# The opening of an FNet and SwiGLU kernel: a warm-up without ScalarE, a first tile negated by VectorE, roots tile by tile, whole first blocks

## The chip, the cores and the metric

The kernel runs on one core of a Trainium2 chip. TensorE multiplies, VectorE and ScalarE do elementwise work, GpSimd does small steps and issues some transfers, and SyncE (SP) issues the others. The metric is the time on the device in microseconds (us), lower is better. Beside it stands one profiled execution, whose trace gives the start and length of each instruction.

## The reference, cut to what matters

```
xn = layernorm(x)                                   # x: 2048 x 640
a, b = xn @ hid_re.T, xn @ hid_im.T                 # DFT along the hidden dimension, 640
s = seq_re @ a - seq_im @ b                         # DFT along the sequence, 2048 (real part)
g = silu((silu(xn @ w_gate) * (xn @ w_up)) @ w_down)   # 640 -> 1536 -> 640
out = x + s * g
```

All is float32.

## The kernel before

The sequence DFT is done first: the two 2048 x 2048 matrices times the normalised rows, result in p_dram. Then the hidden DFT (y_dram), then the feed-forward part in two halves of the sequence, and the product with y and the sum with x at the end. Each of the large products is one level of Strassen's scheme: seven products p1 to p7 of quarter matrices, plus the products d1 to d3 for the last 128 of the 640 columns.

A float32 product is made of faster ones: each operand is split into a rounded high part (ScalarE copies it to a type called fp32r) and a low part (VectorE subtracts the high part from the original). Each 128x128 by 128x512 product is then three matmuls: high by high, high by low, low by high (`mm3`). Only the first products of the opening take unsplit float32 operands.

All work is collected in a `Plan`: matmul groups are steps at planned times from 0 on, and everything else is given a planned time ahead of, or behind, the step that it serves. `schedule` sorts all this; `place` then gives each buffer an address in one of the arenas hl (split operands), raw (everything else) and raw2, by trying five orders of the buffers and several distances in time, `fit` placing one buffer after another. Instructions are then issued in planned order. Each engine works through its own list in order, so a planned time decides what stands ahead of what on an engine, and an instruction that waits holds up those behind it.

The opening (`opening`, within `seq`) covers the first eight row tiles (kk = 0 to 7, 128 rows each). For each tile kk it has two groups of products: the real block (i = 0) and the imaginary block (i = 1) of the sequence DFT, each with three matmul targets, two of p1 and one of d1. For tile 0 they are unsplit: the right operand is `neg`, the negated first 256 columns of the tile, and the tile's own last 128 columns. From tile 1 on each group is nine matmuls. Which block comes when is written by hand:

- the transfers, all in SP's list: x tile 0, first half of real block 0, x tile 1, first half of imaginary block 0, then the two second halves, x tiles 2 and 3, and so on; a half block is 256 KB, a block 512 KB (two k tiles of 128x512), an x tile 320 KB;
- `OPEN_LN`: planned times for the layer norm of tiles 0, 1, 2 with 3, 4 with 5, 6 with 7: statistics on VectorE, a square root on ScalarE, five small steps on VectorE (a reciprocal, then a Newton step that gives the reciprocal root r, then the shift mr), then the normalisation in place on ScalarE;
- `OPEN_T` and `OPEN_S`: planned times for the splits of the right operands (per tile) and of the left ones (per block).

Before all that, z is cleared, ScalarE applies one square root to an element of z, so that its table is loaded, and sixteen matmuls of z with itself (`busy`) run ahead of the first real one. They keep TensorE at work while the first data come in.

Of the kernel before, what the change touches and what calls it, by code (L numbers as in the profile page):

```python
# [11 lines left out]
AF = mybir.ActivationFunctionType  # L12
ALU = mybir.AluOpType

P = 128
S, D, F = 2048, 640, 1536
TC = 512
# [79 lines left out]
class Plan:  # L97
# [97 lines left out]
    def place(self, limits, last):  # L195


        self.ops.sort(key=lambda o: o[:2])
        life = {}
        for i, (t, _, _, names, end) in enumerate(self.ops):  # L200
            for n in names:
                if n in self.size:
                    v = life.setdefault(n, [t, i, end, i])
                    v[2:] = max(end, v[2]), i
        where = {}
        turn = max(v[3] for n, v in life.items() if self.size[n][0] == "raw2")
        free = max(v[2] for n, v in life.items() if self.size[n][0] == "raw2")
        back = next(i for i, o in enumerate(self.ops) if o[0] >= self.back)
        for arena, limit in limits.items():
            wall = {"hl": [(limit, limit + last[0], turn, free + 1, 1e9), (limit + last[0], limit + sum(last), turn, free + 1, back)],  # L210
                    "raw": [(limit, limit + last[1], back, self.back + 2, 1e9)]}.get(arena, [])
            limit = max([limit, *(w[1] for w in wall)])
            mine = [(n, self.size[n][1], *v) for n, v in life.items() if self.size[n][0] == arena]
            orders = (
                lambda m: (m[2], m[3]),
                lambda m: (m[4] - m[2] < 60, m[2], m[3]),
                lambda m: (m[4] - m[2] < 60, -m[1], m[3]),
                lambda m: (-m[1], m[3]),
                lambda m: (m[2] - m[4], m[3]),
            )  # L220
            pauses = (8, 6, 4, 3, 2, 1, 0, -1, -2, -4, -8)
            tries = ((pauses[a:], o) for a in range(len(pauses)) for o in orders)
            found = [f for f in (self.fit(sorted(mine, key=o), limit, p, wall) for p, o in tries) if f]
            if not found:
                raise ValueError(f"{arena}: no room")
            best = min(found, key=lambda f: f[0])
            order, latest = best[3], best
            for _ in range(24):
                hurt = sorted((n for n in latest[2] if latest[2][n] > 9), key=lambda n: -latest[2][n])
                moved = {n: i for i, n in enumerate(hurt[:6])}  # L230
                order = sorted(order, key=lambda m: moved.get(m[0], 99))
                latest = next((f for f in (self.fit(order, limit, pauses[a:], wall) for a in range(len(pauses))) if f), None)
                if latest is None:
                    break
                best = min(best, latest, key=lambda f: f[0])
            where |= best[1]
        return where, turn + 1, back
# [33 lines left out]
def tile_fnet_swiglu(  # L271
# [278 lines left out]
    def xn_tiles(k, n, a=0, w=D):  # L550
        return space["xn", k // 8].rearrange("p (k d) -> p k d", d=D)[:, k % 8:k % 8 + n, a:a + w]
# [7 lines left out]
    def layer_norm(k0, n, lead, root, stats, small):  # L559

        for k in range(k0, k0 + n):
            for h in range(2):
                pl.prod(stats[k - k0], lambda k=k, h=h: nc.vector.bn_stats(
                    bst[:, k % 2, h], xn_tile(k)[:, h * 320:h * 320 + 320]), [(xn, k)], [("bst", k % 2, h)])
            pl.prod(stats[k - k0], lambda k=k: nc.vector.bn_aggr(
                mv[:, k], bst[:, k % 2].rearrange("p a b -> p (a b)")),
                [("bst", k % 2, 0), ("bst", k % 2, 1)], [("mv", k)])  # L570
        y, t, mr, v, nm = (sm[:, i, k0:k0 + n] for i in range(5))
        mean, var = (mv[:, k0:k0 + n, i] for i in range(2))
        r = rowst[:, 0, NS + k0:NS + k0 + n]
        key = ("sm", k0)
        if small is nc.vector:
            stt = small.scalar_tensor_tensor
            ops = [
                lambda: nc.scalar.activation(t, var, AF.Sqrt, bias=sm[:, 5, :1]),
                lambda: small.reciprocal(y, t),
                lambda: stt(t, var, EPS, y, op0=ALU.add, op1=ALU.mult),  # L580
                lambda: stt(t, t, -0.5, y, op0=ALU.mult, op1=ALU.mult),
                lambda: stt(r, t, 1.5, y, op0=ALU.add, op1=ALU.mult),
                lambda: stt(mr, mean, -1.0, r, op0=ALU.mult, op1=ALU.mult),
            ]
        else:
            ops = [
                lambda: small.tensor_scalar(v, var, EPS, 1.0, op0=ALU.add, op1=ALU.mult),
                lambda: small.tensor_tensor(y, v, sm[:, 5, 8:8 + n], op=ALU.pow),
                lambda: small.tensor_scalar(nm, mean, -1.0, 0.0, op0=ALU.mult, op1=ALU.add),
                lambda: small.tensor_tensor(t, v, y, op=ALU.mult),  # L590
                lambda: small.tensor_tensor(t, t, y, op=ALU.mult),
                lambda: small.tensor_scalar(t, t, -0.5, 1.5, op0=ALU.mult, op1=ALU.add),
                lambda: small.tensor_tensor(r, y, t, op=ALU.mult),
                lambda: small.tensor_tensor(mr, nm, r, op=ALU.mult),
            ]
        for i, fn in enumerate(ops):
            pl.prod(root[i > 0], fn, [("mv", k) for k in range(k0, k0 + n)], [key])
        for k in range(k0, k0 + n):
            pl.prod(lead[k - k0], lambda k=k: nc.scalar.activation(
                xn_tile(k), xn_tile(k), AF.Identity, bias=sm[:, 2, k:k + 1], scale=rowst[:, 0, NS + k:NS + k + 1]),  # L600
                [key, (xn, k)], [(xn, k, c) for c in range(3)])
# [86 lines left out]
    def more():  # L688
# [9 lines left out]


    OPEN_LN = ((0, 1, -4.0, -2.8, -2.6, (-1.4,)), (1, 1, -1.4, 0.0, 0.3, (1.4,)), (2, 2, 2.2, 5.8, 5.9, (7.0, 9.0)),  # L700
               (4, 2, 10.5, 13.0, 13.1, (14.2, 17.0)), (6, 2, 18.5, 21.0, 21.1, (22.5, 25.0)))
    OPEN_T = {1: 2.4, 2: 8.0, 3: 10.1, 4: 15.2, 5: 18.0, 6: 23.5, 7: 26.2}
    OPEN_S = {(0, 1): (0.2, 1.6), (1, 1): (0.8, 3.9), (0, 2): (4.6, 7.2), (1, 2): (8.7, 9.4), (0, 4): (13.5, 14.5),
              (1, 4): (15.8, 16.8), (0, 6): (21.5, 22.5), (1, 6): (24.0, 25.2)}
    ahead = {}

    def seq(k):
# [112 lines left out]
        def opening():  # L820
# [16 lines left out]
                else:  # L837
                    pl.prod(at(t), lambda: nc.sync.dma_start(raw(name, a * TC, TC), src[:, a]), [], [(name, a)])

            t = -8.0  # L840
            for what in ((0,), (0, 0, 0), (1,), (1, 0, 0), (0, 0, 1), (1, 0, 1), (2,), (3,), (0, 1), (1, 1), (4,), (5,), (0, 2), (1, 2),
                         (6,), (7,), (0, 3), (1, 3)):
                if len(what) == 1:
                    load_x(what[0], at(t), nc.sync)
                else:
                    fetch(what[0], what[1], t, *what[2:])
                t += 0.45
            for k0, n, stats, root, rest, apply in OPEN_LN:
                layer_norm(k0, n, [at(x) for x in apply], (at(root), at(rest)), [at(stats + i) for i in range(n)], nc.vector)
            neg = pl.buf(("neg",), "raw", 256)  # L850
            pl.prod(at(-0.5), lambda: nc.scalar.activation(
                raw(neg).unsqueeze(1), xn_tiles(0, 1, 0, 256), AF.Copy, scale=-1.0), [(xn, 0, 0)], [(neg, 0)])
            for kk in range(1, 8):
                for r, late in (("p1", 0), ("d1", 0.4)):
                    LEAD["T" + r, kk] = 0, at(OPEN_T[kk] + late), at(OPEN_T[kk] + late + 0.5)
# [469 lines left out]
    found, turn, back = pl.place({"hl": HL_KB * 256, "raw": RAW_KB * 256 - 8, "raw2": TURN_KB * 512}, (TURN_KB * 256, TURN_KB * 256))  # L1325
    where.update(found)

    nc.gpsimd.memset(sm[:, 5, :8], EPS)
    nc.gpsimd.memset(sm[:, 5, 8:], -0.5)
    nc.gpsimd.memset(z, 0.0)  # L1330
    nc.scalar.activation(z[:, :1], z[:, :1], AF.Sqrt)
    started = False
    first, last = ExitStack(), ExitStack()
    for i, stack in enumerate((first, last)):
# [1 line left out]
    for i, (t, _, fn, names, _) in enumerate(pl.ops):  # L1336
        if i == turn:
            last.close()
            first.close()
            space["hl2"], space["hl3"] = (stack.enter_context(tc.tile_pool(name=name, bufs=1, reuse_waits="tile")).tile(  # L1340
                [P, TURN_KB * 256], F32R, name=name) for stack, name in ((ctx, "hl2"), (last, "hl3")))
        if i == back:
            last.close()
            space["raw3"] = ctx.enter_context(tc.tile_pool(name="raw3", bufs=1, reuse_waits="tile")).tile(
                [P, TURN_KB * 256], F32, name="raw3")
        if t >= 0 and not started:
            started = True
            busy(ps[:, 7], 16)
        fn()


# [38 lines left out]
```

## Time and profile before

| | us |
|---|---|
| median of 3 runs (fastest to slowest) | 971.04 (971.01 to 1213.72) |
| the profiled execution, its own time | 971.28 |
| its span, first to last instruction | 969.5 |
| first warm-up matmul | 2.28 |
| first real matmul | 8.39 |
| first matmul on split operands | 13.14 |

The span is what the trace covers; the profiled execution's own time is 1.8 us longer. All rows are in microseconds from the start of the span, unless a column says ns. PE is TensorE, PEld its weight loads, DVE VectorE, ACT ScalarE, POOL GpSimd, and SPq SyncE's issue of transfers. Nearly every instruction is recorded by a helper, so all have line L82, and the tile names tell them apart: xn is the row tiles, sm and rowst the small per-row numbers of the layer norm, raw the plain buffers, hl the split ones, ps the accumulators, in_cs the sequence DFT matrices.

### The profile page before, as it was taken

To read this page: it belongs to the slowest core of one execution; us is meant where nothing else is said; L and a number is where in the kernel's file an instruction comes from. 1 tells how busy PE (TensorE), PEld (TensorE's weight loads), DVE (VectorE), ACT (ScalarE), POOL (GpSimd) and SP (SyncE) were. 2 spreads that over 40 slices of the span, in tenths; PEclk is the share of its full clock that TensorE was granted. 3 is DMA by queue.
4 is the path that set the end of the run, shared out by engine and by line. 5 is a ranking of instruction groups with operands and counts; after the bars stand their busy time and mean duration, and the time that the engine had idled before them with its cause. 6 is when DMAs were issued, how large, how long until landed. Compare 5 with 4: busy or idle time off the path is not lost.

```text
span 969.5 us, 11543 instructions
## 1 busy us (share of the span) xinstructions
PE 962.3 (99%) x4240; PEld 792.9 (82%) x4240; DVE 733.9 (76%) x927; ACT 489.3 (50%) x676; POOL 119.5 (12%) x179
## 2 busy tenths in 40 slices
PE   9999999999999999999999999999999999999997
PEld 5888888888888888888888888888888888888886
DVE  6899688666874687685987888999977666667774
ACT  5786455454555446544346556563445444444341
POOL 0460220011101110111100211210002100000000
PEclk9999999999999999999999999999999999999999
DMA  9998858395838488678573474438688511105593
GB/s 338 289 228 260 220 178 229 114 255 140 212 126 247 136 218 297 155 202 233 160 220 124 159 267 155 168 135 285 227 276 251 145 55 55 37 18 194 196 363 125
DMA packets 64344, 186.50 MB, mean 192 GB/s; under 512 B 6560, under 2 KB 10400, under 8 KB 64288
## 3 DMA queue, kind: packets, MB, share of 16 engines
q1 hardware_dynamic: 46240, 125.45, 38.3%
q0 software_dynamic: 18048, 60.32, 24.4%
q8 instruction: 33, 0.54, 0.2%
q14 instruction: 23, 0.19, 0.1%
HBM read 151.39 MB, written 34.36 MB: 192 GB/s over the span
## 4 chain that ended last, share of the span: by engine, by line
PE 99%; ACT 0%; DVE 0%; issue 0%
PE ps L82 99%; ACT L82 0%; DVE raw L82 0%; ACT raw L82 0%; ACT z L82 0%
## 5 line engine op out<-in xcount | busy, mean ns | idle before, releaser
L82 PE MATMUL ps<-hl 128*128 128x512 f32 (+1 forms) x3277 | 787.9, 388 | 0.0
L82 PEld LDWEIGHTS ps<-hl 128*128 128x128 f32 x3277 | 613.9, 188 | 127.0 <-issue 0.2
L82 DVE TENSOR_TENSOR hl<-raw,hl 128x1024 fp32r<-128x1024 f32 (+5 forms) x360 | 346.6, 994 | 137.2 <-ACT hl L82 92.9
L82 ACT ACTIVATE hl<-raw 128x1024 fp32r<-128x1024 f32 (+6 forms) x416 | 325.8, 826 | 169.2 <-DVE raw L82 91.7
L82 PE MATMUL ps<-hl,hl 128*128 128x512 f32 (+1 forms) x935 | 257.5, 388 | 0.0
L82 ACT ACTIVATE raw<-ps 128x512 f32<-128x512 f32 (+1 forms) x144 | 97.7, 681 | 235.3 <-PE ps L82 230.6
L82 DVE TENSOR_TENSOR raw<-raw 128x256 f32<-128x256 f32 (+7 forms) x236 | 193.0, 843 | 18.3 <-ACT raw L82 15.2
L82 PEld LDWEIGHTS ps<-hl,hl 128*128 128x128 f32 x935 | 175.3, 188 | 36.1
L82 DVE TENSOR_TENSOR raw<-ps,raw 128x512 f32<-128x512 f32 (+1 forms) x95 | 77.2, 814 | 50.9 <-PE ps L82 50.1
L82 ACT ACTIVATE hl<-xn 128x1024 fp32r<-128x1024 f32 (+3 forms) x61 | 42.4, 723 | 13.0 <-PE ps L82 10.2
L82 POOL DMA_DIRECT2D p_dram<-raw x24 | 16.4, 685 | 248.5 <-DVE raw L82 210.3
L82 ACT ACTIVATE raw<-raw 128x512 f32<-128x512 f32 (+1 forms) x30 | 21.5, 718 | 45.9 <-DVE raw L82 44.6
L82 DVE TENSOR_TENSOR hl<-xn,hl 128x1024 fp32r<-128x1024 f32 (+3 forms) x50 | 40.8, 833 | 3.6 <-PE ps L82 3.5
L82 POOL DMA_DIRECT2D raw<-in_cs x36 | 32.2, 987 | 77.6 <-DMA raw<-in_cs 45.6
L82 DVE SCALAR_TENSOR_TENSOR hl<-raw,hl 128x256 fp32r<-128x256 f32 (+4 forms) x56 | 32.8, 586 | 4.2 <-ACT hl L82 4.2
L82 POOL DMA_DIRECT2D out<-raw x10 | 6.9, 685 | 225.0 <-DVE raw L82 189.4
L82 DVE TENSOR_TENSOR raw<-raw,raw 128x512 f32<-128x512 f32 (+3 forms) x30 | 29.0, 973 | 4.7 <-ACT raw L82 4.1
L82 POOL DMA_DIRECT2D d_p<-hl x28 | 15.2, 543 | 71.3 <-ACT hl L82 60.1
L82 DVE BATCH_NORM_STATS2 bst<-xn 128x6 f32<-128x320 f32 x32 | 13.7, 480 | 5.0 <-DMA xn<-in_x 5.0
L82 POOL DMA_DIRECT2D y_dram<-raw x12 | 8.2, 682 | 64.8 <-DVE raw L82 46.4
L82 POOL DMA_DIRECT2D raw<-in_xt x6 | 6.9, 1210 | 72.1 <-DVE raw L82 72.1
L82 ACT ACTIVATE xn<-xn,sm,rowst 128x640 f32<-128x640 f32 x16 | 14.2, 912 | 3.0 <-DVE sm L82 2.0
(38 smaller groups left out, 86.7 us busy)
## 6 DMA issues: line engine op xcount, KB each, us to landing
raw<-in_cs SPq DMA_DIRECT2D x82, 512.0 KB, 6.0
hl<-d_p SPq DMA_DIRECT2D x56, 384.0 KB, 5.2
raw<-in_cs POOLq DMA_DIRECT2D x36, 512.0 KB, 9.2
raw<-in_wb SPq DMA_DIRECT2D x24, 640.0 KB, 4.2
d_p<-hl POOLq DMA_DIRECT2D x28, 384.0 KB, 3.4
p_dram<-raw POOLq DMA_DIRECT2D x16, 512.0 KB, 3.7
raw<-p_dram SPq DMA_DIRECT2D x8, 768.0 KB, 6.9
xn<-in_x SPq DMA_DIRECT2D x16, 320.0 KB, 8.8
```

The lines of the kernel that those rows point to most:

```text
L82: return real(*args, **kw)
```

## The change

The opening is rewritten in five places.

1. z is cleared first, and ScalarE's first square root reads and writes a small tile instead of z. The dummy matmuls wait for the memset alone, and there are eleven of them.
2. For tile 0, VectorE subtracts the mean and multiplies with the negative reciprocal root, straight from the loaded tile, into `neg`; the last 128 columns get the same with the positive root, in place; ScalarE normalises the first 512 columns later. The separate sign flip on ScalarE is gone.
3. Tiles 0 to 3 get their roots one by one. ScalarE computes t, half the root of var + eps; GpSimd computes (var + eps) / 4; VectorE takes the reciprocal of t, one combined step, and a second reciprocal that gives r. Tiles 4 to 7 keep the old steps in pairs.
4. Blocks 0 are fetched whole, and SP's list is two entries shorter.
5. The planned times of the opening are new, and `place` gets additional orders for the case that none of the old ones finds room.

```diff
             found = [f for f in (self.fit(sorted(mine, key=o), limit, p, wall) for p, o in tries) if f]
+            for w in range(25, 425, 25) if not found else ():
+                order = sorted(mine, key=lambda m: (m[4] - m[2] < 60, m[2] < w, m[2], m[3]))
+                found += [f for f in (self.fit(order, limit, pauses[a:], wall) for a in range(len(pauses))) if f]
...
-        if small is nc.vector:
+        if small is nc.vector and n == 1:
+            sign, half = (-1.0, nm) if k0 == 0 else (1.0, r)
+            ops = [
+                lambda: nc.scalar.activation(t, var, AF.Sqrt, bias=sm[:, 5, 4:5], scale=0.25),
+                lambda: nc.gpsimd.tensor_scalar(v, var, EPS, 0.25 * sign, op0=ALU.add, op1=ALU.mult),
+                lambda: small.reciprocal(y, t),
+                lambda: small.scalar_tensor_tensor(v, v, y, t, op0=ALU.mult, op1=ALU.subtract if k0 == 0 else ALU.add),
+                lambda: small.reciprocal(half, v),
+            ]
+            if k0:
+                ops.append(lambda: small.scalar_tensor_tensor(mr, mean, -1.0, r, op0=ALU.mult, op1=ALU.mult))
+        elif small is nc.vector:
...
+        if k0 == 0:
+            neg = pl.buf(("neg",), "raw", 256)
+            minus = lambda to, a, n, scale: small.tensor_scalar(to, xn_tile(0)[:, a:a + n], mean, scale, op0=ALU.subtract, op1=ALU.mult)
+            for e in range(2):
+                pl.prod(root[2], lambda e=e: minus(raw(neg, e * P, P), e * P, P, nm), [(xn, 0), key], [(neg, 0)])
+            pl.prod(root[2], lambda: small.tensor_scalar(r, nm, -1.0, 0.0, op0=ALU.mult, op1=ALU.add), [key], [key])
+            pl.prod(root[2], lambda: minus(xn_tile(0)[:, TC:], TC, P, r), [(xn, 0), key], [(xn, 0, 2)])
+            pl.prod(root[2], lambda: small.tensor_tensor(mr, mean, nm, op=ALU.mult), [key], [key])
+            pl.prod(lead[0], lambda: nc.scalar.activation(
+                xn_tile(0)[:, :TC], xn_tile(0)[:, :TC], AF.Identity, bias=mr, scale=r), [key, (xn, 0), (neg, 0)], [(xn, 0, 0), (xn, 0, 1)])
+            return neg
...
-    OPEN_LN = ((0, 1, -4.0, -2.8, -2.6, (-1.4,)), (1, 1, -1.4, 0.0, 0.3, (1.4,)), (2, 2, 2.2, 5.8, 5.9, (7.0, 9.0)),
-               (4, 2, 10.5, 13.0, 13.1, (14.2, 17.0)), (6, 2, 18.5, 21.0, 21.1, (22.5, 25.0)))
-    OPEN_T = {1: 2.4, 2: 8.0, 3: 10.1, 4: 15.2, 5: 18.0, 6: 23.5, 7: 26.2}
-    OPEN_S = {(0, 1): (0.2, 1.6), (1, 1): (0.8, 3.9), (0, 2): (4.6, 7.2), (1, 2): (8.7, 9.4), (0, 4): (13.5, 14.5),
+    OPEN_DMA = ((0,), (0, 0), (1,), (1, 0), (2,), (3,), (0, 1), (1, 1), (4,), (5,), (0, 2), (1, 2), (6,), (7,), (0, 3), (1, 3))
+    OPEN_LN = ((0, 1, (-2.5,), (-1.4, -1.0, -0.5), (0.4,)),
+               (1, 1, (0.5,), (1.6, 1.9), (2.8,)),
+               (2, 1, (3.4,), (4.5, 4.9), (5.7,)),
+               (3, 1, (6.6,), (7.65, 9.3), (10.1,)),
+               (4, 2, (10.5, 11.5), (13.0, 13.1), (14.2, 17.0)),
+               (6, 2, (18.5, 19.5), (21.0, 21.1), (22.5, 25.0)))
+    OPEN_T = {1: 3.7, 2: 6.7, 3: 11.0, 4: 15.2, 5: 18.0, 6: 23.5, 7: 26.2}
+    OPEN_S = {(0, 1): (-1.1, 2.8), (1, 1): (1.3, 5.8), (0, 2): (4.7, 7.6), (1, 2): (7.7, 10.2), (0, 4): (13.5, 14.5),
...
-            t = -8.0
-            for what in ((0,), (0, 0, 0), (1,), (1, 0, 0), (0, 0, 1), (1, 0, 1), (2,), (3,), (0, 1), (1, 1), (4,), (5,), (0, 2), (1, 2),
-                         (6,), (7,), (0, 3), (1, 3)):
+            t = -6.0
+            for what in OPEN_DMA:
...
-            neg = pl.buf(("neg",), "raw", 256)
-            pl.prod(at(-0.5), lambda: nc.scalar.activation(
-                raw(neg).unsqueeze(1), xn_tiles(0, 1, 0, 256), AF.Copy, scale=-1.0), [(xn, 0, 0)], [(neg, 0)])
...
-    nc.gpsimd.memset(sm[:, 5, :8], EPS)
+    nc.gpsimd.memset(z, 0.0)
+    nc.gpsimd.memset(sm[:, 5, :4], EPS)
+    nc.gpsimd.memset(sm[:, 5, 4:8], 0.25 * EPS)
     nc.gpsimd.memset(sm[:, 5, 8:], -0.5)
-    nc.gpsimd.memset(z, 0.0)
-    nc.scalar.activation(z[:, :1], z[:, :1], AF.Sqrt)
+    nc.scalar.activation(sm[:, 0, :1], sm[:, 5, :1], AF.Sqrt)
...
-            busy(ps[:, 7], 16)
+            busy(ps[:, 7], 11)
```

## Rows read from the trace of the kernel before

**Rows 1.** The page: busy time, share of the span and instructions of each engine.

```profile
PE 962.3 (99%) x4240; PEld 792.9 (82%) x4240; DVE 733.9 (76%) x927; ACT 489.3 (50%) x676; POOL 119.5 (12%) x179
```

**Rows 2.** Waits of PE: us in total, times, longest us.

```profile
PE ps L82 <- ACT z L82: 2.3, 1, 2.3
```

**Rows 3.** Order of time on PE: start, us, engine, operation, count, idle time before.

```profile
2.28 6.27 PE L82 MATMUL ps<-z 128*128 128x512 bf16 x16 [2.28 <-ACT z L82]
8.39 1.88 PE L82 MATMUL ps<-raw 128*128 128x512 f32 x4
...
13.14 373.46 PE L82 MATMUL ps<-hl 128*128 128x512 f32 x1645
```

**Rows 4.** Order of time, all engines, first 14 us: the clearing and use of z.

```profile
0.80 0.53 POOL L82 MEMSET z<- 128x512 bf16 x1
...
2.02 0.20 ACT L82 ACTIVATE z<-z 128x1 bf16<-128x1 bf16 x1
```

**Rows 5.** Order of time, first 14 us: weight loads of the last warm-up matmuls.

```profile
7.38 0.15 PEld L82 LDWEIGHTS <-z 128*128 128x128 bf16 x1 [0.28 <-issue]
7.74 0.31 PEld L82 LDWEIGHTS <-z 128*128 128x128 bf16 x2 [0.21 <-issue]
```

**Rows 6.** Order of time, first 14 us: tile 0, from its landing to its negated copy.

```profile
3.54 0.89 DVE L82 BATCH_NORM_STATS2 bst<-xn 128x6 f32<-128x320 f32 x2 [3.54 <-DMA xn<-in_x]
...
4.71 0.29 ACT L82 ACTIVATE sm<-mv,sm 128x1 f32<-128x1 f32 x1 [2.48 <-DVE mv L82]
...
5.04 0.16 DVE L82 RECIPROCAL sm<-sm 128x1 f32<-128x1 f32 x1 [0.36 <-ACT sm L82]
...
5.82 0.16 DVE L82 SCALAR_TENSOR_TENSOR sm<-mv,rowst 128x1 f32<-128x1 f32 x1
...
6.96 0.42 ACT L82 ACTIVATE raw<-xn 128x256 f32<-128x256 f32 x1
```

**Rows 7.** Groups by form, first 40 us: count, busy us, mean ns, idle before.

```profile
L82 DVE TENSOR_TENSOR hl<-xn,hl 128x128 fp32r<-128x128 f32 x8 | 2.2, 273 | 0.0
...
L82 DVE TENSOR_TENSOR hl<-raw,hl 128x512 fp32r<-128x512 f32 x2 | 1.4, 688 | 0.3 <-ACT hl L82 0.3
```

**Rows 8.** Order of time on POOL: small layer norm steps of later tiles.

```profile
42.20 0.18 POOL L82 TENSOR_SCALAR sm<-mv 128x2 f32<-128x2 f32 x1 [1.90 <-DVE mv L82]
...
43.99 1.04 POOL L82 TENSOR_SCALAR sm<-sm 128x2 f32<-128x2 f32 x1
```

**Rows 9.** Order of time, first 14 us: what waited for transfers, and tile 1.

```profile
6.37 0.89 DVE L82 BATCH_NORM_STATS2 bst<-xn 128x6 f32<-128x320 f32 x2 [0.40 <-DMA xn<-in_x]
...
8.44 0.63 ACT L82 ACTIVATE hl<-raw 128x512 fp32r<-128x512 f32 x1 [0.61 <-DMA raw<-in_cs]
...
10.04 0.63 ACT L82 ACTIVATE hl<-raw 128x512 fp32r<-128x512 f32 x1 [0.96 <-DMA raw<-in_cs]
...
10.57 0.91 ACT L82 ACTIVATE xn<-xn,sm,rowst 128x640 f32<-128x640 f32 x1
...
10.83 0.89 DVE L82 BATCH_NORM_STATS2 bst<-xn 128x6 f32<-128x320 f32 x2 [1.03 <-DMA xn<-in_x]
...
11.96 0.42 DVE L82 SCALAR_TENSOR_TENSOR hl<-xn,hl 128x256 fp32r<-128x256 f32 x1
```

**Rows 10.** Stretches: us, busy us (instructions) by engine, PE clock, DMA share, GB/s.

```profile
5.00:10.00 5.00, 5.00 (x15) 2.06 (x13) 3.40 (x14) 2.26 (x5) 0.00 (x0) 1.00 0.97 263
10.00:15.00 5.00, 5.00 (x16) 2.72 (x15) 3.94 (x14) 3.30 (x6) 0.00 (x0) 1.00 1.03 418
```

**Rows 11.** Order of time, 14 to 30 us: low parts for tile 2.

```profile
16.59 0.43 DVE L82 SCALAR_TENSOR_TENSOR hl<-xn,hl 128x256 fp32r<-128x256 f32 x1 [0.31 <-ACT hl L82]
...
17.75 1.23 DVE L82 TENSOR_TENSOR hl<-raw,hl 128x1024 fp32r<-128x1024 f32 x1 [0.53 <-ACT hl L82]
```

**Rows 12.** Waits of SP's own queue: us in total, times, longest us.

```profile
SPq L82 <- DVE hl L82: 284.3, 45, 25.8
```

**Rows 13.** The page, DMA issues: count, KB each, us to landing.

```profile
raw<-in_cs SPq DMA_DIRECT2D x82, 512.0 KB, 6.0
```

More of the change, by code (lines that the diff above doesn't have):

```diff
@@ L847, in opening @@
                 t += 0.45
-            for k0, n, stats, root, rest, apply in OPEN_LN:
-                layer_norm(k0, n, [at(x) for x in apply], (at(root), at(rest)), [at(stats + i) for i in range(n)], nc.vector)
-            neg = pl.buf(("neg",), "raw", 256)
-            pl.prod(at(-0.5), lambda: nc.scalar.activation(
-                raw(neg).unsqueeze(1), xn_tiles(0, 1, 0, 256), AF.Copy, scale=-1.0), [(xn, 0, 0)], [(neg, 0)])
+            neg = [layer_norm(k0, n, [at(x) for x in apply], [at(x) for x in root], [at(x) for x in stats], nc.vector)
+                   for k0, n, stats, root, apply in OPEN_LN][0]
             for kk in range(1, 8):
```

## The prediction

> **What bounds the kernel now.** I read three views in this order. First the busy times of the page: TensorE is busy for 962.3 of 969.5 us, and no other engine comes near [rows 1]. A busy matmul row alone doesn't prove a bound, so the second view is what the matmuls waited for: over the whole execution there is one wait, 2.3 us at the start, for ScalarE [rows 2]. Third, the order of time on TensorE: warm-up matmuls from 2.28, the first real ones from 8.39, and from 13.14 products of split operands that follow each other without a gap [rows 3]. So the time is 8.39 us of opening, then some 956 us of unbroken matmuls, then a tail of about 5 us. The change touches the opening. Whatever it brings is at most what lies ahead of 8.39, and it counts in full only if the matmuls behind find their operands that much earlier as well.
>
> What fills the 8.39 us: ScalarE loads its table, and its first activation, in place on z, ends at 2.22; z itself was written by 1.33 [rows 4]. Sixteen warm-up matmuls follow, 0.43 us apart (512 columns in 0.43 us is the 1.2 GHz level); the weight loads close up from 0.43 to under 0.4 us at 7.74, which is where the 2.4 GHz level begins [rows 5]. That is about 5.4 us after the first of them. Meanwhile the first tile's negated copy is ready at 6.96 + 0.42 = 7.38 [rows 6]. So the real matmuls start when the warm-up ends, 1 us after their operands exist.
>
> **The change, part by part.** *Warm-up.* The dummy matmuls need only z. Its memset takes 0.53 us [rows 4] and now goes first in GpSimd's list, so they start at about 1.35, 0.9 us earlier. Eleven at 0.43 us end at 6.05.
>
> *First operand.* It no longer passes through ScalarE's normalisation and sign flip. VectorE subtracts the mean and multiplies by the negative root itself. From the square root's end at 5.00 [rows 6]: reciprocal, one combined step, reciprocal, each 0.16 us as there and 0.2 us from start to start, until 5.6; then two subtractions of 128x128, for which the nearest row is a 128x128 tensor operation of 0.27 us [rows 7]. That makes 6.15, 1.2 us earlier than 7.38. The added GpSimd step (variance plus eps) runs beside the square root. Its nearest rows are 0.18 us and, beside a VectorE operation, 1.04 us [rows 8]. At 4.7 VectorE waits for ScalarE, as it does in the first of those rows, so I take 0.18 and it is hidden; at 1.04 it would end at 5.75 and the operand would come 0.5 us later.
>
> *First left operand.* The first seq-DFT block is now fetched as one 512 KB transfer instead of its first half. Landing times of before, by the engines that waited for them: x tile 0 at 3.54 [rows 6], x tile 1 at 6.37, the second half of block 0 at 8.44, the second half of the imaginary block 0 at 10.04, x tile 2 at 10.83 [rows 9]. In the order of issue these stand after 320, 896, 1408, 1664 and 1984 KB. The whole block 0 now stands at 832 KB: between 3.54 and 6.37 that is 6.06; at the 418 GB/s of the later stretch [rows 10] it is 4.8. Either is ahead of 6.15. So the first real matmul can start at 6.2 against 8.39, 2.2 us earlier.
>
> *Clock.* If the faster level again comes 5.4 us after the first dummy, that is 6.75, and the stretch from 6.2 to 6.75 runs at half pace: it costs 0.3 us. If it came at 7.7 as before, it would cost 0.75; if before 6.2, nothing. I take 0.3. The first three unsplit products are six records of 0.43 us, 2.56 us, so they end at 6.2 + 2.56 + 0.3 = 9.05.
>
> *Second left operand.* The next three products need the imaginary block 0, now whole, at 1664 KB. By the bytes of before it lands at 10.04; at 418 GB/s, 1376 kB after 3.54, at 6.85. The 5 to 10 us stretch moved 263 GB/s [rows 10], which gives 8.8. I take that, as it is the stretch in question. Then TensorE doesn't wait: 9.05 + 2.56 = 11.6 against about 13.5 before, where twelve records from 8.39 end.
>
> *Second tile.* Here I expect most of the gain to be lost. ScalarE works in order, and its new list puts the split of the imaginary block (now 0.63 us, after the landing) ahead of the square root of tile 1; before, that root was ahead of both splits. So: split 8.8 to 9.45, root from 9.45. Then from the root's start to the shift's end took 4.71 to 5.98 for tile 0 [rows 6] with five VectorE steps, now four: 1.1 us, to 10.55. Normalising takes 0.91 [rows 9], to 11.5, and the rounded (high) part of its right operand 0.42, as the flip of the same size did [rows 6]: 11.9. On VectorE the low part of the same operand stands behind the low part of block 0 (0.69 [rows 7], to 11.25) and behind the statistics of tile 2 (10.83 to 11.96 before, 1.15 us to the next operation [rows 9], so to 12.4), and takes 0.42: 12.8. The third matmul of the group needs it, 0.45 us after the first, so the group runs as if started at 12.35. Against 13.5 the gain is 1.15 us. The root's fewer steps are worth 0.2 us per tile, and only for tile 1 do they lie on this path. Tiles 2 and 3, now one by one, add five small steps (1 us) to VectorE, which was busy 3.4 and 3.9 of each 5 us [rows 10].
>
> *Behind that.* The tightest operands of the old opening are the low part of tile 2's right operand, ready at 17.02 for a matmul at 18.05, and the low part of the next imaginary block, ready at 18.98 for 19.85 (start of the second tile's group at 13.5 plus two or three groups of nine matmuls at 0.227 us, 2.04 each, plus one or two matmuls) [rows 3, 11]. They have 1.0 and 0.9 us. A gain of 1.15 us therefore asks little more of them than they had, and both chains begin earlier now, tile 2's without waiting for tile 3. I cost this at nothing; if they didn't move at all, the gain would end at 0.9.
>
> Sum: -1.15 us on the profiled execution of 971.28 us, which lies 0.24 above the median of the runs shown; from that median, 971.04, I get **969.9**.
>
> **Rivals.** *The transfers decide.* The block lands no earlier than 10.04 by bytes and tile 2 not before 10.83. Then the split ends at 10.7, the root's chain at 11.8, the high part at 13.15, the low part at 14.0; the group runs as from 13.6 and nothing is gained: 971.0. For it: the DMA was as busy in 5 to 10 us as later, yet slower [rows 10]. Against it: those were 256 KB pieces; whole blocks ran at 418 GB/s.
>
> *The best case.* The block lands near 7 and the clock rises early. Then TensorE alone decides, 6.2 + 5.12 = 11.3, a gain of 2.2: 968.8. Against it: the statistics of tile 2 ahead of tile 1's low part.
>
> *The clock (slower).* Before, TensorE worked without a break from 2.28 to the rise, and on. Now eleven dummies end at 6.05, perhaps before the rise, and any pause until the operand, or until the second block, interrupts that work. If the 5.4 us then start anew at 6.2, the products up to 11.6 run at half pace and lose 2.7 us: they end at 14.0, 0.5 us later than before, 971.5. It decides as soon as the pause resets the rise. Against it: the pause I compute is 0.15 us. The Trainium skill, "TensorE: Matmul & The Clock Gate", section "What's actually happening", speaks against shortening the warm-up: it says that the monitor runs freely and isn't reset by the kernel's start, so that the rise comes at a varying moment. By that rule the price would differ from run to run between 0 and the 0.75 us above, and the runs before should scatter too; two agree within 0.03 us, so I give it little.
>
> *Placement (slower).* The planner gets additional orders for the case that no old order finds room; if one of them is used, buffers of the whole kernel change place, and some transfer is issued only when its buffer comes free. The SP queue already waited 284.3 us in 45 waits for VectorE to be done with a buffer, 6.3 us each [rows 12], without TensorE noticing. A block needs 6.0 us from issue to landing [rows 13], and 1.2 us for its low part [rows 11]: a buffer that comes free less than about 7 us before its use stops TensorE. A few such cases at 1 to 2 us give 973 or so.
>
> **Numbers.** Forecast (gain 0.5 to 2.2, its own range 968.8 to 970.5, best case within): 0.60. Transfers decide, 970.5 to 971.2: 0.20. Clock, 971.5: 0.06. Placement, 971.2 to 975, seldom far more: 0.12. Still faster: 0.02. The range 968.8 to 971.6 leaves out the last and most of placement. A measurement tells about 2% (19 us) from no change; the opening has only 8.39 us to give, so faster by that much is all but excluded (0.01), slower needs many placement stalls (0.02), within 2% 0.97.
>
> **What would show it.** The first dummy near 1.35, the first unsplit product near 6.2, the first split product between 11.9 and 12.4, no matmul waits behind it. A weight-load pace of 0.85 us among the unsplit products would be the clock; a ScalarE split that waits for its block until 10 the transfers; TensorE gaps behind 60 us placement.

## The result and the profile after

The changed kernel takes 974.17 us (median of 8 runs, 973.58 to 974.73) against 971.02 for the kernel before: ratio 1.0032, 95% interval 1.0021 to 1.0044. It is 3.1 us slower. One of the eight runs of the kernel before took 1213.72 us, which nothing on record explains, and the ratio leaves it out. The prediction had it 1.1 us faster, with 968.8 to 971.6 as its range.

First the order of time on TensorE after, to be read against [rows 3] (start, us, then the instruction):

```profile
1.30 4.68 PE L82 MATMUL ps<-z 128*128 128x512 bf16 x11 [1.30 <-POOL sm L82]
6.48 1.98 PE L82 MATMUL ps<-raw 128*128 128x512 f32 x4 [0.49 <-DVE raw L82]
...
9.25 1.98 PE L82 MATMUL ps<-raw 128*128 128x512 f32 x4
...
12.41 47.82 PE L82 MATMUL ps<-hl 128*128 128x512 f32 x208 [0.32 <-ACT hl L82]
```

The dummies start 1 us earlier, the first real matmul 1.9 us earlier, the split products 0.7 us earlier. So in this pair of executions the opening did what it was meant to do. The waits of TensorE in the whole execution (us in total, times, longest), against the single one of [rows 2]:

```profile
PE ps L82 <- DVE hl L82: 2.5, 1, 2.5
PE ps L82 <- POOL sm L82: 1.3, 1, 1.3
PE ps L82 <- DVE raw L82: 0.5, 1, 0.5
PE ps L82 <- ACT hl L82: 0.3, 1, 0.3
```

Three of the four belong to the opening. The first doesn't. It lies at 743 us, where the second half's gate products begin. Among VectorE's waits stands one that the kernel before doesn't have, for output transfers:

```profile
DVE raw L82 <- DMA out<-raw: 6.8, 2, 5.9
```

The order of time there, all engines:

```profile
728.62 1.24 POOL L82 DMA_DIRECT2D raw<-in_xt  x1 [21.29 <-DVE raw L82]
...
739.46 0.74 POOL L82 DMA_DIRECT2D out<-raw  x1 [9.60 <-DMA raw<-y_dram]
...
743.25 0.61 PE L82 MATMUL ps<-hl,hl 128*128 128x512 f32 x2
744.54 0.83 DVE L82 TENSOR_TENSOR raw<-raw 128x640 f32<-128x640 f32 x1 [5.86 <-DMA out<-raw]
...
745.89 0.42 DVE L82 SCALAR_TENSOR_TENSOR hl<-raw,hl 128x256 fp32r<-128x256 f32 x1
...
746.36 4.38 PE L82 MATMUL ps<-hl,hl 128*128 128x512 f32 x11 [2.50 <-DVE hl L82]
```

VectorE stands idle for 5.86 us, until an output transfer that GpSimd issued at 739.46 has landed. That transfer waits in turn for the one issued at 728.62, which adds x to what stands in the same buffer (an accumulating transfer). The view puts this wait to a load of y; but the output instruction itself waits on the semaphore of the accumulating transfer, which landed at 739.2, 0.3 us earlier, and in the kernel before the two stand 0.3 us apart as well. VectorE's next operation forms the weight sums of the first column block, and behind it in VectorE's order stands the low part that TensorE's third matmul of this stage needs. In the kernel before, the same VectorE operation (there merged with the one after it) doesn't wait, although the output transfer was issued at the same time:

```profile
739.18 1.42 DVE L82 TENSOR_TENSOR raw<-raw 128x640 f32<-128x640 f32 x2
739.58 0.74 POOL L82 DMA_DIRECT2D out<-raw  x1 [9.07 <-DMA raw<-in_xt]
```

The stretches after (us, busy us and instructions of PE, PEld, DVE, ACT, POOL, then PE's granted clock, DMA share, GB/s):

```profile
743.00:746.00 3.00, 0.86 (x4) 0.38 (x2) 1.46 (x3) 0.60 (x2) 0.00 (x0) 1.00 0.98 157
746.00:750.00 4.00, 3.64 (x9) 2.92 (x10) 4.00 (x8) 3.76 (x7) 1.66 (x2) 0.57 0.35 114
750.00:754.00 4.00, 4.00 (x20) 3.21 (x19) 4.00 (x9) 2.51 (x6) 0.28 (x1) 1.00 0.50 109
```

TensorE issues 4 matmuls in the 3 us of the gap and 9 in the next 4 us at a granted clock of 0.57. The kernel before has 15 and 19 there.

To see what is left of the opening just before this, take one VectorE operation, the same in both kernels, first of before, then of after:

```profile
724.25 1.22 DVE L82 TENSOR_TENSOR hl<-raw,hl 128x1024 fp32r<-128x1024 f32 x1
```

```profile
723.61 1.22 DVE L82 TENSOR_TENSOR hl<-raw,hl 128x1024 fp32r<-128x1024 f32 x1
```

The changed kernel is 0.64 us ahead at 724 us. Matmul by matmul (both traces have all 4212 products on split operands) it then loses 2.66 us in the gap and 1.72 us behind it, so the last matmul comes 3.74 us later; the tail behind the last matmul is 0.75 us shorter in this execution, and the span is 3.0 us longer (972.5 against 969.5).

Why the two kernels differ at 743 us, with no code changed there: the new planned times of the opening change how long its buffers live, and `place` then finds another arrangement. For the hl arena none of the five old orders finds room any more, and one of the additional orders is used. For the raw arena the arrangement that the kernel before had no longer fits, and the next best is taken. In it the result buffers of three quarters of the first half's down product (12, 22 and 21) are reused 2.0 to 3.4 us of planned time after their planned end; in the kernel before nothing follows any of them within 8.8 us. These buffers wait for an accumulating transfer on GpSimd's queue and then for the output transfer, and both land later than the planner assumes: it counts 4.4 and 3.4 us from issue to landing, and for quarter 12 they took 10.6 and 5.0.

### The profile page after: what moved, and what is told of

Read it like the earlier page. It is cut to its first block, busy times and chain, and to the rows that moved or that the text cites. A ratio compares the mean times of both kernels' runs of the same rounds, so it can differ in the third digit from the quotient of the medians.

```text
span 972.5 us, 11526 instructions
## 1 busy us (share of the span) xinstructions
PE 963.7 (99%) x4235; PEld 792.6 (81%) x4235; DVE 734.0 (75%) x932; ACT 488.7 (50%) x676; POOL 120.2 (12%) x184
## 4 chain that ended last, share of the span: by engine, by line
PE 93%; issue 4%; DMA 1%; POOL 0%; DVE 0%; ACT 0%; SPq 0%; POOLq 0%; DVEq 0%
PE ps L82 93%; DMA raw<-in_cs 1%; DMA out<-raw 1%; POOL raw L82 0%; DVE raw L82 0%; SPq L82 0%; ACT xn L82 0%; POOL out L82 0%; DVE sm L82 0%; ACT hl L82 0%; DVE hl L82 0%; ACT raw L82 0%; ACT sm L82 0%; DVE rowst L82 0%; POOLq L82 0%
## 5 line engine op out<-in xcount | busy, mean ns | idle before, releaser
L82 DVE TENSOR_TENSOR raw<-raw 128x1024 f32<-128x1024 f32 (+6 forms) x233 | 193.9, 856 | 28.0 <-ACT raw L82 13.5
L82 PEld LDWEIGHTS ps<-hl,hl 128*128 128x128 f32 x945 | 178.3, 189 | 39.9 <-DVE hl L82 2.9
L82 DVE TENSOR_TENSOR raw<-raw,raw 128x256 f32<-128x256 f32 (+3 forms) x33 | 28.4, 866 | 5.5 <-ACT raw L82 5.1
L82 ACT ACTIVATE xn<-xn,sm,rowst 128x640 f32<-128x640 f32 (+1 forms) x16 | 14.2, 908 | 5.0 <-DVE sm L82 3.4
```

Of the source, the lines that this page charges most:

```text
L82: return real(*args, **kw)
```

## The experiments

Each comparison is with runs of the kernel before taken beside it on the same chip, so the time of that kernel is given with it.

**One buffer moved in the changed kernel.**

```diff
     where.update(found)
+    where["fin", 0, 12, 0, 0] = 14336
```

> The changed kernel with one address changed: the result buffer of quarter 12 of the first half's down product is put at word 14336 of the raw arena, which is free for its whole life, instead of at word 6528, where the weight sums of the second half's first column block are written next. Theory (the address costs the time): VectorE no longer waits 5.86 us for the output transfer, TensorE's gap of 2.66 us at 743 us and the slow matmuls behind it (1.7 us) go, nothing else changes: 974.2 - 4.4 = 969.8 us, and the opening's gain of 0.64 us over the kernel before is left, plus what its tail differs. Rival (the earlier opening makes TensorE run ahead of its transfers, whatever the addresses): the wait turns up at another buffer at about the same place, and the time stays at 973 to 974.5.

Measured: 973.71 us against 971.25, ratio 1.0026 (1.0015 to 1.0037). The 5.86 us wait at 744 is gone, yet most of the loss stayed, as the rival had it. In the profiled execution three gaps, of 0.7 to 0.8 us lost at each, took its place: one at 731, for a load of the down product's d3 operand, and two at 750 and 770. One row of its order of time shows where the last comes from:

```profile
765.04 1.76 DVE L82 TENSOR_TENSOR raw<-raw 128x512 f32<-128x512 f32 x3 [4.91 <-DMA out<-raw]
```

It is the same kind of wait at another of the three buffers. So the theory in the form "this address costs the time" fell. What remained was a wider one, all three buffers, or the rival.

**The same overlap put into the kernel before.**

```diff
     where.update(found)
+    where["fin", 0, 12, 0, 0] = 1536
```

> The kernel before with one address changed: the same result buffer is put at word 1536 of the raw arena, where the weight sums of the second half's first column block follow it, as in the changed kernel. The opening is the old one. Theory (the address alone costs the time): a gap of 2 to 3 us on TensorE at about 744 us, matmuls at half pace behind it, 971.0 + 4.4 = 975.4 us. Rival (only together with the new opening): no gap, 971.0.

Measured: 973.72 us against 971.25, ratio 1.0022 (1.0013 to 1.0032). With the old opening and one address changed the wait appears:

```profile
742.89 1.43 DVE L82 TENSOR_TENSOR raw<-raw 128x640 f32<-128x640 f32 x2 [4.36 <-DMA out<-raw]
...
744.71 2.60 PE L82 MATMUL ps<-hl,hl 128*128 128x512 f32 x10 [0.94 <-DVE hl L82]
...
748.57 0.50 PE L82 MATMUL ps<-hl,hl 128*128 128x512 f32 x1 [1.26 <-ACT raw L82]
```

TensorE loses 1.1 and 1.4 us in the two gaps, 2.5 in all, and the clock stays at full level. The mechanism doesn't need the new opening. The size expected, 4.4, was that of the changed kernel with its longer gap: here the output transfer landed at 742.8, there at 744.5.

**The warm-up alone, in the kernel before.**

```diff
+    nc.gpsimd.memset(z, 0.0)
     nc.gpsimd.memset(sm[:, 5, :8], EPS)
     nc.gpsimd.memset(sm[:, 5, 8:], -0.5)
-    nc.gpsimd.memset(z, 0.0)
-    nc.scalar.activation(z[:, :1], z[:, :1], AF.Sqrt)
+    nc.scalar.activation(sm[:, 0, :1], sm[:, 5, :1], AF.Sqrt)
...
-            busy(ps[:, 7], 16)
+            busy(ps[:, 7], 14)
```

> The kernel before with the warm-up part alone: z cleared first, ScalarE's first root on another tile, fourteen dummy matmuls. No planned time and no address changes. The first dummy at 1.30, the operand of tile 0 at 7.4 as before, so real matmuls from 7.4 to 7.5 instead of 8.39; the low part of tile 1's right operand is ready at 12.38 and is needed at about 13.0. Theory (most of the opening's gain comes from the warm-up): 971.0 - 0.95 = 970.1 us. Rival (the warm-up brings nothing without the rest, since the transfers and tile 1 decide): 970.9 to 971.1.

Measured: 970.80 us against 971.25, ratio 0.9996 (0.9987 to 1.0004). The medians differ by half of what was expected, and the interval takes in no change and the 0.95 us alike: inconclusive. Nor can its trace decide. It is 0.43 us ahead of the kernel before's at 724 us, but the trace of the run just above, whose opening is the old one, is 0.73 us ahead there.

**The moved buffer and the root ahead of the split.**

```diff
-    OPEN_S = {(0, 1): (-1.1, 2.8), (1, 1): (1.3, 5.8), ...
+    OPEN_S = {(0, 1): (-1.1, 2.8), (1, 1): (1.7, 5.8), ...
```

> The changed kernel with the moved buffer of the first of these runs and one planned time: ScalarE's split of the imaginary block 0 goes behind the square root of tile 1 (1.7 instead of 1.3). The addresses are those of the first run. Theory (ScalarE's order holds tile 1 back): the root starts at 8.3 instead of 9.77, tile 1 is normalised by 10.8, the split groups start when the unsplit products end at 11.8 instead of 12.6, 0.6 to 0.8 us less than the first run, 969.1 us. Rival (transfers and VectorE hold it): within 0.2 us of the first run.

Measured: 973.19 us against 971.25, ratio 1.0021 (1.0012 to 1.0030), 0.5 us under the run with the moved buffer alone, which the intervals don't separate. Its profiled execution loses 2.41 us at 749 (2.63 from one matmul's start to the next), and this time the view names the transfer at once, on ScalarE:

```profile
751.10 1.09 ACT L82 ACTIVATE raw<-ps 128x512 f32<-128x512 f32 x2 [3.73 <-DMA out<-raw]
```

ScalarE wants to empty an accumulator into the buffer that follows quarter 22's, the second of the three pairs. In the run with one moved buffer the same instruction had waited too, but was put down to TensorE, which had long been done. The opening of this execution shows nothing of the theory: the imaginary block landed only at 10.1, and the first split product came at 12.46, against 12.37 in the run with one moved buffer.

**All three buffers moved.**

```diff
     where.update(found)
+    for i, q in enumerate((12, 22, 21)):
+        where["fin", 0, q, 0, 0] = 14336 + 1024 * i
```

> The changed kernel with three addresses changed: the result buffers of the quarters 12, 22 and 21 of the first half's down product go to words 14336, 15360 and 16384 of the raw arena, free for 20 us of planned time behind their planned end. In the changed kernel the next buffers (weight sums, two copies of accumulators, a product) follow them 2.0 to 3.4 us behind it; in the kernel before, none within 8.8 us. Theory (output transfers that land later than planned hold these three places): no TensorE gap after 20 us, and the opening's gain of 0.64 us is left, against the kernel before 0.9993, about 970.6. Rival (the planner's new addresses cost in many more places, or the earlier opening itself does): further gaps at other times, 972 to 974.

Measured: 970.13 us against 971.47, ratio 0.9986 (0.9978 to 0.9995). Each against the kernel before beside it, three addresses take 4.5 us off the changed kernel (1.0032 to 0.9986), and it is now faster than the kernel before. The same stretches as above, of this kernel:

```profile
743.00:746.00 3.00, 3.00 (x15) 2.46 (x14) 2.31 (x4) 2.32 (x4) 0.00 (x0) 1.00 0.89 156
746.00:750.00 4.00, 4.00 (x19) 3.34 (x18) 4.00 (x8) 2.21 (x5) 1.66 (x2) 1.00 0.33 132
```

TensorE is busy throughout both at full clock. VectorE and ScalarE no longer wait for an output transfer, though that of quarter 12 lands about as late as in the changed kernel (744.0 against 744.5). Over all experiments, the traces with such a wait are those of the kernels above 973 us, and no other trace has one. This settles the cause: all other new addresses, those of the hl arena included, stay here as they are in the changed kernel. One part of the expectation missed: a short wait is left, the one for the load of the d3 operand, at 731.

```profile
PE ps L82 <- DMA hl<-d_d: 0.2, 1, 0.2
```

It costs 0.4 us here and 1.0 us in the last run below; there is none in the kernel before or after. Neither the new hl addresses nor the earlier TensorE alone brings it: the two runs with one buffer moved, without and with the root, have the same addresses and are equally far ahead there (0.68 and 0.66 us), and only the one without waits. Its four d3 loads took 4.4 us to land (median), those of the other 3.7. What delays them stays open.

**Three buffers and the root ahead of the split.** The two edits above together.

> The three moved buffers, and ScalarE's split of the imaginary block 0 behind the square root of tile 1. Theory (ScalarE's order holds tile 1 back): 0.3 to 0.6 us less than with the three buffers alone, about 970.1. Rival (the landing of the blocks, which differs by a microsecond from execution to execution, decides): the same as with the three buffers alone within 0.2 us.

Measured: 969.47 us against 971.47, ratio 0.9982 (0.9973 to 0.9991), the fastest version of the study. It is 0.66 us under the three buffers alone. The intervals overlap, though the step goes the same way and by about the same amount as with one moved buffer. Its profiled execution, at 971.02 the slowest of its runs, shows what the clock rival of the prediction costs. First TensorE's order of time, then weight loads:

```profile
1.31 4.87 PE L82 MATMUL ps<-z 128*128 128x512 bf16 x11 [1.31 <-POOL sm L82]
6.74 3.75 PE L82 MATMUL ps<-raw 128*128 128x512 f32 x4 [0.56 <-DMA raw<-in_cs]
10.29 1.23 PE L82 MATMUL ps<-raw,xn 128*128 128x512 f32 x2
```

```profile
9.43 0.34 PEld L82 LDWEIGHTS ps<-raw,xn 128*128 128x128 f32 x1 [0.52 <-DVE sm L82]
10.29 0.34 PEld L82 LDWEIGHTS ps<-raw,xn 128*128 128x128 f32 x1 [0.52 <-issue]
```

The records of the unsplit products stand 0.86 us apart, at the 1.2 GHz level, until about 10.7 us: four of them take 3.75 us instead of 1.98, and the first split product comes at 13.52. It is the only trace that shows a wait of TensorE between its first matmul and the rise of the clock. That fits the rival's condition, a pause that puts the rise off; with one such trace it isn't shown.

**Three buffers, and the warm-up behind ScalarE again.**

```diff
-    nc.scalar.activation(sm[:, 0, :1], sm[:, 5, :1], AF.Sqrt)
+    nc.scalar.activation(z[:, :1], z[:, :1], AF.Sqrt)
```

> The three moved buffers, and the warm-up waits for ScalarE's first root on z again: eleven dummies from 2.28 instead of 1.30, so the real matmuls from 7.0 at the earliest instead of 6.5. Theory (tile 1's operand decides when the split groups start, not the first matmul): the unsplit products end by 12.1, the split groups start at 12.4 to 12.6 all the same, equal to the three buffers alone within 0.2 us. Rival (the start of the first matmul decides): 0.5 us more.

Measured: 970.25 us against 971.47, ratio 0.9986 (0.9977 to 0.9995), the same as without this edit. In the profiled execution the first dummy comes at 2.28, the first split product at 12.32 (12.16 with the three buffers alone):

```profile
2.28 4.01 PE L82 MATMUL ps<-z 128*128 128x512 bf16 x11 [2.28 <-ACT z L82]
...
12.32 7.93 PE L82 MATMUL ps<-hl 128*128 128x512 f32 x32 [0.32 <-ACT hl L82]
```

Once tile 1 decides, the warm-up without ScalarE brings nothing that these runs show. This profiled execution can't prove it for every one, since here the dummies took only 4.01 us.

**The gap filled with dummies in the changed kernel.**

```diff
         nc.tensor.matmul(o, w(0), m(1), start=False, stop=False, skip_group_check=True)
+        busy(ps[:, 4], fill)          # fill = 12 in the first gate product of the second half, else 0
```

> The changed kernel, with twelve dummy matmuls (2.56 us at the fast pace) into an unused accumulator bank between the second and the third matmul of the second half's first gate product, where TensorE has its gap; addresses as in the changed kernel. Theory (the gap lets the clock fall, and that costs 1.7 us on top of the gap): the gap is filled, no matmuls at half pace behind it, 974.2 - 1.7 = 972.5. Rival (the clock's fall isn't due to the gap, or costs nothing since other waits follow): 974.2. Where the gap is short in an execution, the dummies cost time instead, up to 2.6 us.

Measured: 974.29 us against 971.47, ratio 1.0031 (1.0022 to 1.0041): nothing gained. The rows of its order of time, and its stretch from 746:

```profile
743.61 2.76 PE L82 MATMUL ps<-z 128*128 128x512 bf16 x12
...
750.21 0.50 PE L82 MATMUL ps<-hl,hl 128*128 128x512 f32 x1 [1.28 <-ACT raw L82]
```

```profile
746.00:750.00 4.00, 2.93 (x12) 1.80 (x10) 4.00 (x8) 3.75 (x7) 1.66 (x2) 1.00 0.38 132
```

The clock no longer falls (1.00 instead of 0.57), and TensorE still arrives at 750.2, because it now waits for ScalarE. Idle for 5.9 us, VectorE had held ScalarE up for 4.9 us, and from 746 on the two work off what piled up, at the same times in both kernels: ScalarE's emptying of the accumulators, first here, then in the changed kernel, ends at 750.2 in both.

```profile
748.67 1.49 ACT L82 ACTIVATE raw<-ps 128x1024 f32<-128x1024 f32 x2
```

```profile
748.68 1.49 ACT L82 ACTIVATE raw<-ps 128x1024 f32<-128x1024 f32 x2
```

The rival won. The half pace in the changed kernel was covered, so in this pair of executions the slow clock added nothing to the loss. Among the eight runs of the changed kernel, the four with the lower mean clock (0.998) took 974.33 to 974.73 us, the others 973.58 to 974.01; whether the clock or a longer gap makes these 0.6 us stays open.

**The planner told of the late transfers.** The root ahead of the split as above, no address set by hand, and in `place`:

```diff
-                    v[2:] = max(end, v[2]), i
+                    v[2:] = max(end + (12 if n[:2] == ("fin", 0) else 0), v[2]), i
```

> The changed kernel, the split of the imaginary block 0 behind the square root of tile 1, and instead of moved addresses one number in the planner: the result buffers of the first half's down product are taken to be in use 12 us longer than planned. All buffers of the raw arena are placed anew. Theory (their late output transfers are what the planner doesn't know): no gap on TensorE in 735 to 775 us, the same time as with the three buffers moved by hand and the root order, 0.998 of the kernel before. Rival (any new set of addresses brings its own waits): gaps elsewhere, above 971.

Measured: 970.39 us against 971.61, ratio 0.9984 (0.9975 to 0.9993). One number in the planner does what the three addresses did. In its profiled execution, with the blocks landing as in the changed kernel, the first split product comes at 11.66 instead of 12.41:

```profile
11.66 8.70 PE L82 MATMUL ps<-hl 128*128 128x512 f32 x35
```

That is what the root's place can be worth. The other two traces with this order don't show it, one for a block that landed late, one for the clock; the medians have it at 0.5 and 0.7 us, which the intervals don't separate.

## Why the prediction was wrong

The opening, which got nearly all of the working, came out close. The dummies were forecast from 1.35 and started at 1.30. Tile 0's operand was forecast for 6.15 and came at 6.48, mostly because tile 0 landed 0.25 us later than before. The imaginary block was forecast for 8.8 and landed at 9.2. The order of ScalarE did hold tile 1 back, as written:

```profile
9.23 0.63 ACT L82 ACTIVATE hl<-raw 128x512 fp32r<-128x512 f32 x1 [1.18 <-DMA raw<-in_cs]
...
9.77 0.28 ACT L82 ACTIVATE sm<-mv,sm 128x1 f32<-128x1 f32 x1
...
10.99 0.92 ACT L82 ACTIVATE xn<-xn,sm,rowst 128x640 f32<-128x640 f32 x1 [0.95 <-DVE sm L82]
```

These rows are from the order of time of the changed kernel: split, root, normalisation, one behind the other. The statistics of tile 1 were done at 8.24, so the root lost 1.5 us to the split. The split products ran as from 12.58, where I had 12.35: 0.96 us gained instead of 1.15. Then the step "Behind that" failed in a small way. I cost the tile 2 operands at nothing, and the group of tile 2 lost 0.32 us, 0.64 being left.

These gains are read against one trace of the kernel before, in which the clock rose late (7.7 us). Here is the old opening, unchanged, in the run with the overlap put into the kernel before (there at 5.2 us):

```profile
2.28 5.06 PE L82 MATMUL ps<-z 128*128 128x512 bf16 x16 [2.28 <-ACT z L82]
7.51 1.98 PE L82 MATMUL ps<-raw 128*128 128x512 f32 x4 [0.18 <-ACT raw L82]
...
12.37 7.88 PE L82 MATMUL ps<-hl 128*128 128x512 f32 x32
```

Its split products start at 12.37, as early as the changed kernel's. So the 0.96 and the 0.64 us are partly the luck of that pair. What the opening is worth rests on the runs with the placement mended, not on a pair of traces.

The step that failed is the placement: it stands in my sum at nothing, and among the rivals at 0.12, and it cost 4.5 us. I named the cause, new addresses for buffers of the whole kernel, expected 971.2 to 975 from it, where the time lies, and had its sign right (TensorE gaps behind 60 us). That is partly luck, for the wait was of another kind than the one I described. I had loads in mind that are issued late for want of a buffer; what happened is that VectorE and ScalarE may not write into a buffer until an output transfer has read it. Three things in my working were wrong.

- I took its condition ("if one of them is used") for unlikely. For the hl arena the additional order was needed, and for the raw arena the lost arrangement was enough, with no new order.
- I looked at the wrong queue. I priced SP's waits and a plain block's 6.0 us [rows 13]. The buffers that mattered wait for GpSimd's accumulating transfer: issued at 728.62 in the changed kernel, it held back the output transfer until 739.46, and that landed only at 744.5. In the kernel before the first step took nearly as long (729.26 to 739.58). The profile of before had these rows; no matmul waited for them, because nothing reused the buffers soon.
- I took "without TensorE noticing" as evidence of slack. It held for the old addresses only.

The chance of the clock rival rested on a wrong reading as well. I let two runs that agreed within 0.03 us speak against a varying moment of the rise. The 31 runs of the kernel before beside the three-buffer run lie between 970.54 and 972.40. In the rows just shown, of the same opening code, sixteen dummies take 5.06 us instead of 6.27 [rows 3], and the first real matmul comes at 7.51 instead of 8.39. So the Trainium skill, "TensorE: Matmul & The Clock Gate", "What's actually happening", was right that the moment varies; it varied by more than the 500 ns either way that the section gives, between 4.3 and 10.7 us over the profiles here. By these rows it is worth up to 0.9 us of the old opening, and 1.8 us in the four slow records above. It doesn't explain the loss, which the three addresses do.

What the parts are worth, as far as measured: the opening, with the placement mended, 1.3 us (0.0014 of the time; 0.5 to 2.1 by the interval), of which the warm-up without ScalarE is no measurable part; the warm-up alone in the kernel before at most 1.3 us; the three addresses 4.5 us against it.

## What to carry to other kernels

Where a planner places buffers, a change of times at one end can move every address, so the place to look for the loss is the whole trace, beginning with the waits of the bounding engine. A buffer that a transfer still reads is in use until that transfer has landed, and the planner has to be given the landing that the trace shows, above all for a transfer that waits for another one. A wait that is removed at one buffer can turn up at the next, so move all the suspects before giving up the theory; and before pricing a slow clock, check whether another engine sets the pace there anyway.

## What the hardware showed that I had not expected

- The moment at which TensorE's faster level begins differed from execution to execution far more than I had allowed: by the pace of the matmuls at 7.7 us in the kernel before, about 5.2 with the overlap put into it, and about 10.7 in the three-buffer run with the root moved.
- A gap of about 2.9 us from the start of one matmul to that of the next, in a stretch that was otherwise dense, was enough for the granted clock to read 0.57 in the following 4 us. One of 2.6 us, in the run with one buffer moved and the root ahead, was too (0.64 from 752 to 756 us). In the runs with one buffer moved and with the overlap put into the kernel before, gaps up to 1.7 us left it at 1.00.
- An accumulating transfer of 512 KB from GpSimd's queue took 10.0 and 10.6 us from issue to landing (kernel before and after), and the output of the same buffer was issued only then. That is no price of accumulating: a plain load of 512 KB of y, issued on SP's queue 1.5 us later, took 9.4 and 9.8 us. The DMA engines were busy throughout that stretch (share 1.0 from 730 to 740 us), and the median block of [rows 13] says little of it.
